# A gated linear attention and a two-layer network on one core: one running sum done by matmuls again, weights loaded in whole quarters, a new order of the work

## The chip, the core and the metric

The kernel runs on one NeuronCore of a Trainium2 chip. The core has five engines that run side by side, each with its own instruction queue: TensorE (PE in the profile, with its weight loads PEld), VectorE (DVE), ScalarE (ACT), GpSimd (POOL) and SyncE (SP), which here only issues DMAs. An instruction waits at the head of its queue until what it needs is there, and holds up whatever is queued behind it. The metric is device time in microseconds, lower is better.

## The reference

For each of 4 batches and 8 heads a state of 48 x 48 is decayed and updated along 768 steps; the result, put together to 3072 rows of 384, goes through two layers.

```python
f = 1 / (1 + exp(-f_logit))                       # q, k, v, f_logit: 4 x 8 x 768 x 48, float32
for t in range(768):
    state = f[:, :, t, :, None] * state + einsum('bhd,bhe->bhde', k[:, :, t], v[:, :, t])
    y[:, :, t] = einsum('bhd,bhde->bhe', q[:, :, t], state)
x = y.transpose(0, 2, 1, 3).reshape(3072, 384)
h = x @ w_in                                      # w_in: 384 x 2048
out = maximum(0.01 * h, h) @ w_out                # w_out: 2048 x 384
```

## The kernel before

The work is cut into twelve units of 256 rows. Units 0 to 3 ("paired") are one batch each, with its first 256 steps, two steps side by side on a partition. Units 4 to 11 are two batches each, with one further chunk of 128 steps. In the names below, a number behind the first one is the half of the unit, or for paired units often the half of the heads.

Attention of a unit: loads `Lf`, `Lk`, `Lq`, `Lv` (SyncE, L164 and L168); `ge` and `gl`, exponential and logarithm on ScalarE (L229, L241), which give the logarithm of the decay; `cs`, its running sum by matmuls with triangles of ones (L250 to L261), followed in a paired unit by four tiny matmuls for the ends; `dec`, exponentials of the running sum with both signs and of its ends (L274 to L280); `k` and `q`, products with these (L286, VectorE or GpSimd as the order's last digit says); then keys and queries are transposed, in units 0 to 2 by TensorE (`tk`, `tq`, L319) and copied out (`ck`, `cq`, L332, L334), in units 3 to 11 by a DMA (`xk`, `xq`, L339). `sc` are the scores (L355, L362), `mk` their mask (L372, L376), `v` the casts of v (L291 to L300), `mx` and `ms` the output with the part that comes from the state (L393), `xt` its copy (L445, L447), `pt` the update of the state (L458, L463), `sf` and `sb` its sums and casts (L473 to L483).

The running sum of a paired unit has two columns of steps. The even one is two matmuls of 192 columns; the odd one is two more, or, for the units in `ADDED`, the even one plus the decay, an addition on VectorE in PSUM (`ca`, L266) ahead of `dec`.

The two layers: `up` (six matmuls of 256 columns for a unit, L510) with `pr` (L516) in units 0 to 3; in units 4 to 11 two units share three matmuls of 512 columns (`uw`, L521, with `pw`, L525). `dn_j_a_n` is a quarter of the second layer for half a unit, four matmuls of 384 columns (L532); `ob` copies the result (L541, L543), `st` stores it. The last unit's second half is done in two halves of columns (`dh`, `oh`, `sh`).

Weights come as quarters of 512 columns (w_in) or rows (w_out) in float32 into four buffers of the raw inputs that units 4 and 5 use later, and are cast to bfloat16. `WI_i` and `WO_i` load quarter i whole, `CI_i_x_e` and `CO_i_x_e` cast a third of it (512 columns of the buffer, on VectorE, ScalarE or GpSimd for e = 0, 1, 2). `We_i_x` loads half a quarter of w_in (256 columns), `Ce_i_x_y_e` casts 128 columns of it. `up_j_g` reads quarter g // 2.

There are eight PSUM banks; the digit behind @ in the order names the bank (or banks) of a TensorE step, and a step waits until the bank's last reader is done. `F_n` are fillers: n matmuls on constants whose result nobody reads.

All of it is issued in one long list of such words, written out from a planner; each engine takes its own words in the order of the list.

Of the kernel before, what the change touches and what calls it, by code (L numbers as in the profile page):

```python
# [15 lines left out]
def kernel(  # L16
# [115 lines left out]
    def fill(n, bank):  # L132
        for _ in range(n):
            nc.tensor.matmul(banks[bank].rearrange("t (a n) -> t a n", a=4), filler,  # L134
                             filler[:, None, :].to_broadcast([128, 4, 128]), start=True, stop=True)
# [452 lines left out]
    sc_0_0@6.2 q_1_1_1 zv_1_1 mk_0_0_0 gl_2_1 F_2@1 cs_2_1@3 q_1_0_0 ca_2_1 F_1@4 tq_1_0@1 dec_2_0 ck_1_0_0 cq_1_0_1
    mk_0_0_1 tq_1_1@4 We_0_0 q_2_0_0 cq_1_1_1 v_1_0 dec_2_1 Lv_2_2 WI_2 F_2@5 sc_1_0@6.7 mx_0_2@5.1 sc_1_1@2.4
    mk_1_0_1 mk_1_0_0 v_1_1 tq_2_0@7 q_2_1_1 mk_1_1_1 mk_1_1_0 xt_0_0_1 ms_0 pt_1_2@3.6 xt_0_1_1 Ce_0_1_0_1  # L590
    Ce_0_1_1_1 F_2@2 mx_1_2@5.4 k_2_0_0 tk_2_0@1 sf_1_0 cq_2_0_0 Ce_0_0_0_1 Ce_0_0_1_1 xt_1_0_1 up_0_1@2 k_2_1_1
    ck_2_0_0 sb_1_0 tq_2_1@3 tk_2_1@7 sf_0_1 v_2_1 v_2_0 We_1_0 up_0_0@1 cq_2_1_1 CI_2_1_2 zs_2_1 ms_1 pr_0_1
# [5 lines left out]
    up_2_7@3 sb_0_1 cs_3_0@0 CO_0_0_2 CO_2_1_2 pr_0_4 CO_2_0_2 gl_3_1 CO_1_2_2 Lf_4_1 CO_1_0_2 pr_2_1 pr_2_2 pr_0_6
    ca_3_0 cs_3_1@7 dec_3_0 pr_2_7 pr_1_6 dn_0_1_0@5 up_2_4@2 up_1_7@6 dn_0_0_0@0 up_2_6@3 Lk_3_2 dn_1_0_0@4 CO_1_1_2
    Lf_5_1 pr_2_4 k_3_0_0 CO_2_2_0 ca_3_1 dec_3_1 Lq_3_2 Lf_5_0 WO_3 dn_0_0_1 q_3_1_1 pr_2_6 CO_3_1_0 k_3_1_1 Lf_4_0  # L600
    dn_1_0_1 dn_1_0_2 dn_0_1_1 dn_1_1_0@2 dn_0_0_2 Lv_3_2 dn_1_1_1 xk_3 sb_1_1 pr_1_7 dn_1_1_2 up_2_5@7 q_3_0_0
    dn_0_1_2 up_0_7@3 CO_3_0_0 v_3_0 sb_2_1 CO_3_2_1 pr_0_7 xq_3 Lq_4_0 v_3_1 Lk_4_0 Lq_5_1 Lk_5_1 Lk_5_0 Lq_5_0
    dn_1_0_3 Lf_6_0 Lf_6_1 Lq_4_1 ob_1_0_0 pr_2_5 ge_4_2 pr_2_0 dn_0_0_3 dn_1_1_3 dn_0_1_3 dn_2_1_0@6 ob_1_1_0
    ob_0_0_0 ge_5_2 gl_5_2 sc_3_1@3.7 sc_3_0@4.1 pt_3_2@2.0 dn_2_1_1 mk_3_0_1 dn_2_1_2 mk_3_0_0 mk_3_1_1 sf_3_0
    mk_3_1_0 cs_5_0@1 dn_2_0_0@4 sb_3_0 cs_5_1@7 dn_2_0_1 dec_5_0 ob_0_1_0 gl_4_2 dec_5_1 mx_3_2@2.1 ms_3 xt_3_1_0
    k_5_2_1 dn_2_0_2 q_5_2_1 Lk_4_1 cs_4_1@3 xk_5 xt_3_0_1 xq_5 up_3_2@5 up_3_5@7 Lv_4_1 pr_3_5 dec_4_1 up_3_6@2
    up_3_1@1 pr_3_1 st_0_0 cs_4_0@7 dec_4_0 ge_6_2 k_4_2_0 sf_3_1 dn_2_0_3 q_4_2_1 Lv_4_0 pr_3_2 up_3_7@3 up_3_0@1
    up_3_4@7 xk_4 pr_3_0 xq_4 up_3_3@0 Lv_5_1 Lv_5_0 sb_3_1 pr_3_6 dn_3_1_0@5 pr_3_3 gl_6_2 Lk_7_1 Lf_7_0 Lq_6_0
    pr_3_4 st_0_1 Lq_6_1 dn_2_1_3 v_4_2 ob_2_0_1 dn_3_1_1 cs_6_0@1 pr_3_7 v_5_2 dec_6_0 Lf_7_1 sc_5_0@2.0 sc_5_1@7.4
    dn_3_1_2 mk_5_0_1 cs_6_1@3 mk_5_0_0 dn_3_0_0@0 dn_3_0_1 st_1_1 mk_5_1_0 sc_4_1@1.2 mk_5_1_1 sc_4_0@7.4 dec_6_1  # L610
    mk_4_1_1 dn_3_0_2 pt_4_0@3 mk_4_1_0 mk_4_0_0 pt_4_1@2 dn_3_1_3 mk_4_0_1 mx_4_1@1 mx_4_0@7 mx_5_1@4 xt_4_1_1
    xt_5_1_1 mx_5_0@1 xt_5_0_1 dn_3_0_3 xt_4_0_0 uw_4_7@7 uw_4_9@4 pt_5_1@1 Lk_6_1 sf_4_1 ob_2_1_1 uw_4_4@2 pw_4_7
    Lf_8_0 Lk_6_0 uw_4_15@6 uw_4_0@7 pw_4_4 sf_4_0 uw_4_10@3 ob_3_1_0 uw_4_3@2 pw_4_9 pw_4_0 q_6_2_1 pw_4_10 ge_7_2
    uw_4_8@4 pt_5_0@7 sf_5_0 uw_4_12@5 uw_4_11@3 pw_4_3 uw_4_1@2 uw_4_2@7 pw_4_15 sb_4_1 gl_7_2 pw_4_8 pw_4_11 xq_6
    Lv_6_1 Lq_7_1 cs_7_1@6 cs_7_0@4 pw_4_1 pw_4_2 dec_7_1 uw_4_6@3 sb_5_0 sb_4_0 Lk_7_0 uw_4_13@2 sf_5_1 Lf_8_1
    Lq_7_0 dec_7_0 pw_4_6 st_1_0 k_6_2_0 pw_4_13 dn_4_1_0@1 uw_4_5@7 xk_6 q_7_2_0 pw_4_5 st_2_1 k_7_2_1 xk_7 Lv_6_0
    xq_7 st_3_1 Lv_7_1 Lv_7_0 ob_3_0_1 Lf_9_0 Lf_9_1 v_6_2 dn_5_0_0@6 dn_4_0_0@4 dn_5_1_0@3 uw_4_14@2 Lq_8_1 ge_8_2
    st_2_0 Lk_9_1 sb_5_1 Lq_8_0 pw_4_12 v_7_2 st_3_0 Lk_8_1 Lq_9_0 Lf_10_0 Lk_8_0 pw_4_14 Lv_9_1 Lq_9_1 gl_8_2
    dn_4_0_1 dn_4_1_1 dn_5_1_1 dn_4_0_2 sc_6_1@7.0 sc_6_0@5.2 Lf_11_1 dn_4_1_2 Lk_9_0 dn_4_1_3 mk_6_1_0 mk_6_1_1
    mk_6_0_1 dn_5_0_1 dn_4_0_3 mk_6_0_0 ob_4_1_0 sc_7_1@7.0 sc_7_0@2.5 cs_8_0@1 dn_5_1_2 dn_5_0_2 Lv_8_1 mk_7_0_1  # L620
    mk_7_0_0 mk_7_1_0 mk_7_1_1 cs_8_1@5 mx_6_1@2 dec_8_1 mx_6_0@7 mx_7_1@0 xt_6_0_0 mx_7_0@5 xt_7_1_0 pt_6_1@7
    xt_6_1_1 xt_7_0_1 sf_6_1 dec_8_0 ge_9_2 sb_6_1 dn_5_0_3 pt_7_0@2 uw_6_14@0 uw_6_0@5 pw_6_0 pw_6_14 gl_9_2
# [58 lines left out]
```

## Time and profile before

| | |
|---|---|
| time, median of 3 runs | 179.84 us (179.12 to 180.2) |
| the profiled execution | 178.5 us, span 176.7 us |
| TensorE busy | 168.0 us, 95% of the span |
| ScalarE, VectorE, GpSimd busy | 107.5, 79.1, 72.7 us |
| HBM read, written | 25.17 MB, 4.72 MB |
| DMA packets | 110,407, of them 102,832 under 512 B |

A row of the page's chain names what the end of the program was waiting for, followed back. A row of groups gives line, engine, operation, tiles, count, busy time and mean nanoseconds of one. A row of the timeline gives start and length in us, and in brackets how long the engine sat idle before it and what ended that. For DMA issues the last number is the time in us from issue to landing.

### The profile page before, as it was taken

How to read it: one execution, taken by the hardware profiler on the slowest of the kernel's cores; microseconds unless marked ns; L12 is line 12 of the kernel's file. 1: busy time of each engine (PE TensorE's matmuls, PEld its weight loads, DVE VectorE, ACT ScalarE, POOL GpSimd, SP SyncE). 2: the span in 40 equal slices, each digit the busy share in tenths (PEclk: the TensorE clock that was granted, in tenths of full speed). 3: DMA queues.
4: the chain of work that ended last, by engine and by line, in shares of the span. 5: the costliest groups of instructions: out<-in, count | busy, mean ns of one | idle time of the engine just before them, and what ended most of it. 6: DMA issues, size and time to landing. Idle time of an engine off the chain costs nothing.

```text
span 176.7 us, 5136 instructions
## 1 busy us (share of the span) xinstructions
PE 168.0 (95%) x2096; PEld 105.6 (60%) x2096; DVE 79.1 (45%) x166; ACT 107.5 (61%) x234; POOL 72.7 (41%) x151
## 2 busy tenths in 40 slices
...
PEclk9999999999999999999999999999999999999999
...
GB/s 148 317 323 342 355 312 353 125 326 209 312 206 210 91 194 177 215 188 200 211 229 233 192 188 216 227 134 212 264 206 225 156 250 0 48 0 137 0 22 156
DMA packets 110407, 34.93 MB, mean 198 GB/s; under 512 B 102832, under 2 KB 109616, under 8 KB 110384
## 3 DMA queue, kind: packets, MB, share of 16 engines
...
HBM read 25.17 MB, written 4.72 MB: 169 GB/s over the span
## 4 chain that ended last, share of the span: by engine, by line
PE 90%; DVE 3%; ACT 2%; DMA 2%; issue 1%; SPq 0%; DVEq 0%
PE ps L532 35%; PE ps L521 22%; PE ps L510 11%; PE ps L393 6%; PE ps L134 3%; PE ps L362 3%; DMA raw_fk<-in_f_logit_dram 2%; PE ps L319 2%; PE ps L548 2%; PE ps L258 1%; DVE wm L372 1%; PE ps L463 1%; PE ps L355 1%; PE ps L458 1%; PE ps L250 1%
## 5 line engine op out<-in xcount | busy, mean ns | idle before, releaser
L532 PE MATMUL ps<-w_out,gT 128*128 128x384 bf16 x368 | 66.1, 326 | 0.9 <-DVE sf L475 0.9
L532 PEld LDWEIGHTS <-gT 128*128 128x128 bf16 x368 | 34.4, 98 | 24.3 <-issue 1.2
L521 PE MATMUL ps<-xT,w_in 128*128 128x512 bf16 x192 | 45.2, 379 | 0.0
L525 ACT ACTIVATE gT<-ps 128x512 bf16<-128x512 f32 x64 | 34.5, 623 | 10.1 <-PE ps L521 9.6
L521 PEld LDWEIGHTS <-w_in 128*128 128x128 bf16 x192 | 18.1, 98 | 18.9
L376 DVE TENSOR_TENSOR wm<-ps,ut 128x512 bf16<-128x512 f32 x32 | 19.9, 684 | 17.0 <-PE ps L362 12.2
L286 POOL TENSOR_TENSOR qh<-raw_qv,at 128x768 bf16<-128x768 f32 (+1 forms) x10 | 14.0, 1404 | 24.3 <-ACT gT L525 9.4
L510 PE MATMUL ps<-xT,w_in 128*128 128x256 bf16 x192 | 22.9, 273 | 0.4 <-ACT xT L445 0.2
L516 ACT ACTIVATE gT<-ps 128x512 bf16<-128x512 f32 x32 | 17.9, 616 | 6.2 <-PE ps L510 6.2
L291 POOL CAST vb<-raw_qv 128x384 bf16<-128x384 f32 (+1 forms) x16 | 11.6, 723 | 23.6 <-DMA raw_qv<-in_v_dram 23.4
L510 PEld LDWEIGHTS <-w_in 128*128 128x128 bf16 x192 | 18.4, 98 | 3.6 <-DVE w_in L189 0.5
L483 POOL CAST sb<-sf 64x192 bf16<-64x192 f32 x40 | 14.9, 374 | 10.8 <-DVE sf L473 8.5
L445 ACT CAST xT<-ps 128x384 bf16<-128x384 f32 x15 | 7.8, 529 | 16.9 <-PE ps L393 13.5
L274 ACT ACTIVATE em<-ps 128x384 bf16<-128x384 f32 x24 | 12.2, 508 | 9.0 <-DVE wm L376 5.5
L229 ACT ACTIVATE e<-raw_fk 128x384 f32<-128x384 f32 (+1 forms) x16 | 11.0, 685 | 8.1 <-DMA raw_fk<-in_f_logit_dram 8.0
L286 DVE TENSOR_TENSOR kh<-raw_fk,em 128x768 bf16<-128x768 f32 (+1 forms) x10 | 9.0, 901 | 14.6 <-ACT em L274 9.7
L475 DVE TENSOR_TENSOR sf<-sf,ps 64x192 f32<-64x192 f32 x32 | 11.2, 351 | 6.4 <-ACT at L275 2.8
L543 DVE COPY osb<-ps 128x384 f32<-128x384 f32 x13 | 7.1, 554 | 13.0 <-PE ps L532 9.0
L275 ACT ACTIVATE at<-ps 128x384 bf16<-128x384 f32 x24 | 12.3, 512 | 0.0
L480 POOL TENSOR_TENSOR sf<-sf,end 128x192 f32<-128x192 f32 x16 | 8.9, 556 | 5.9 <-DVE sf L475 5.6
L372 DVE TENSOR_TENSOR wm<-ps,pair_mask 128x512 bf16<-128x512 f32 x16 | 10.4, 685 | 1.8 <-ACT lf L241 0.9
L134 PE MATMUL ps<-filler 128*128 128x512 bf16 x24 | 9.2, 511 | 2.0 <-DVE filler L93 1.1
(90 smaller groups left out, 180.2 us busy)
## 6 DMA issues: line engine op xcount, KB each, us to landing
...
raw_fk<-in_moe_w_out_dram SPq DMA_DIRECT2D x2, 768.0 KB, 7.2
raw_qv<-in_moe_w_out_dram SPq DMA_DIRECT2D x2, 768.0 KB, 5.0
raw_fk<-in_f_logit_dram SPq DMA_DIRECT2D x3, 384.0 KB, 4.7
```

What stands on the lines that cost most here:

```text
L134: nc.tensor.matmul(banks[bank].rearrange("t (a n) -> t a n", a=4), filler, filler[:, None, :].to_broadcast([128, 4, 128]), start=True, sto ...
L274: nc.scalar.activation(ems[j % 2][:, a], t[:, 0:H * D], AF.Exp, scale=1.0)
L275: nc.scalar.activation(ats[j % 2][:, a], t[:, 0:H * D], AF.Exp, scale=-1.0)
L286: eng.tensor_mul(heads(j, to[j % NR], a)[:, :, :, 0:D], raw_heads(j, x, a), decays(j, by, a))
L372: nc.vector.tensor_mul(w.rearrange("t (s p) n -> t s p n", s=2), src.rearrange("t (s p n) -> t s p n", s=2, p=2), pair_mask[:, :, None, :] ...
L376: nc.vector.tensor_mul(w, src.rearrange("t (p n) -> t p n", p=P2), ut[:, None, :].to_broadcast([128, P2, 128]))
L483: nc.gpsimd.tensor_copy(out=sb[rows, :, y * D:y * D + D], in_=sf[rows])
L510: nc.tensor.matmul(pm[:, i, :], w_in_of(ff, kk), xTs[j // 2 % 2][:, kk, j % 2].rearrange("t a s -> t (a s)"), start=(kk == 0), stop=(kk == ...
L516: nc.scalar.activation(dst, pm, AF.Prelu, alpha=0.01)
L521: nc.tensor.matmul(banks[bank], w_in_of(ff, kk), xTs[j // 2 % 2][:, kk].rearrange("t u a s -> t (u a s)"), start=(kk == 0), stop=(kk == NK ...
L525: nc.scalar.activation(g_blocks(j)[ff], banks[st[j].pop(("pm", ff))], AF.Prelu, alpha=0.01)
L532: nc.tensor.matmul(po, g_of(j, ff, a), w_out_b[quarter][:, ff % 4, :], start=(ff == 0), stop=(ff == NF - 1))
```

## The change

Four things change, and nothing else in the functions:

- `ADDED` loses unit 2: its odd running sums are matmuls again, and the words `ca_2_0` and `ca_2_1` are gone.
- Every quarter of w_in is loaded and cast whole: no `We` and `Ce`, four `WI` and twelve `CI`, in the order 0, 3, 1, 2.
- A filler has 256 columns instead of 512, and there are 35 (16, 8, 4, 5, 2) instead of 24.
- The list is a new one from end to end: other places, other banks, and in part other engines for the copies and products.

```diff
-    ADDED, WIDE = (2, 3), (4, 6, 8, 10)
+    ADDED, WIDE = (3,), (4, 6, 8, 10)
...
-            nc.tensor.matmul(banks[bank].rearrange("t (a n) -> t a n", a=4), filler,
-                             filler[:, None, :].to_broadcast([128, 4, 128]), start=True, stop=True)
+            nc.tensor.matmul(banks[bank][:, 0:256].rearrange("t (a n) -> t a n", a=2), filler,
+                             filler[:, None, :].to_broadcast([128, 2, 128]), start=True, stop=True)
...
-    c0 Lf_0_1 ge_0_1 Lf_1_2 ge_1_1 gl_0_1 ge_1_0 zk_0 zv_0_0 zs_0_0 Lv_0_1 Lf_0_0 F_7@1 cs_0_1@0 ge_0_0 gl_0_0 Lk_0_1
-    Lv_0_0 zk_2 dec_0_1 v_0_1 Lq_0_1 Lk_0_0 Lq_0_0 zk_1 F_3@2 cs_0_0@1 zs_1_0 Lk_1_2 gl_1_0 gl_1_1 k_0_1_0 F_3@3
-    cs_1_0@2 Lf_2_2 dec_0_0 q_0_1_0 k_0_0_0 pm_1 tk_0_1@3 tq_0_1@4 cs_1_1@5 dec_1_0 v_0_0 tk_0_0@6 ck_0_1_0 Lq_1_2
-    Lq_2_2 cq_0_1_0 dec_1_1 Lv_1_2 Lk_2_2 zv_2_0 pt_0_2@7.0 q_0_0_1 sc_0_1@1.3 k_1_0_1 ge_2_0 We_0_1 tq_0_0@2 k_1_1_1
...
-    xt_1_1_1 ut Ce_1_0_0_2 ck_2_1_0 sc_2_0@5.0 sc_2_1@3.7 sf_1_1 pr_0_0 mk_2_1_0 CI_2_0_1 pt_2_2@2.6 CI_2_2_0
-    up_1_1@4 mk_2_0_1 sf_2_0 up_1_0@1 mk_2_1_1 Ce_1_0_1_1 pr_1_1 pr_1_0 mk_2_0_0 up_0_5@3 up_1_5@0 We_1_1 Lf_3_2
-    sb_2_0 WI_3 up_1_4@2 up_0_2@4 mx_2_2@7.1 WO_0 CI_3_1_2 ms_2 xt_2_1_0 Ce_1_1_1_0 xt_2_0_1 up_1_2@5 up_0_4@7
-    Ce_1_1_0_0 pr_1_5 pr_1_2 WO_2 pr_1_4 CI_3_2_2 zs_3_0 ge_3_0 pr_0_2 WO_1 up_0_3@1 ge_3_1 CI_3_0_0 up_2_3@0
...
-    uw_6_6@6 pw_6_6 pw_6_13 dn_6_1_0@7 pw_6_8 uw_6_10@0 dn_6_0_0@2 uw_6_9@6 uw_6_7@4 dec_9_1 pw_6_5 q_9_2_0 q_8_2_1
-    xk_8 xq_8 k_9_2_0 xk_9 pw_6_10 uw_6_11@5 pw_6_11 pw_6_7 pw_6_9 dn_7_1_0@1 dn_7_0_0@3 uw_6_15@0 Lv_9_0 xq_9
...
+    c0 zs_0_1 Lf_0_1 Lf_0_0 zv_0_0 Lf_1_2 Lv_0_0 Lv_0_1 Lk_0_1 ge_0_1 gl_0_1 ge_0_0 zk_1 zk_2 zs_1_1 zk_0 Lq_0_1
+    gl_0_0 pm_1 ge_1_0 ge_1_1 F_16@1 cs_0_1@0 Lq_0_0 dec_0_1 k_0_1_0 cs_0_0@1 dec_0_0 Lk_0_0 gl_1_1 F_8@3 tk_0_1@2
+    gl_1_0 q_0_1_0 v_0_0 v_0_1 F_4@4 cs_1_0@3 tq_0_1@4 cs_1_1@5 k_0_0_1 zv_2_1 Lk_1_2 Lf_2_2 cq_0_1_1 dec_1_0 dec_1_1
+    Lq_1_2 ck_0_1_0 q_0_0_0 zv_1_1 k_1_0_1 tk_0_0@6 ck_0_0_0 k_1_1_1 tq_0_0@7 sc_0_1@0.1 pt_0_2@2.4 cq_0_0_0 mk_0_1_1
+    sc_0_0@6.3 sf_0_0 ge_2_0 ge_2_1 mk_0_1_0 Lv_1_2 q_1_1_0 F_5@7 tk_1_1@7 gl_2_0 tk_1_0@1 gl_2_1 sb_0_0 Lk_2_2
+    ck_1_0_1 cs_2_0@5 v_1_0 v_1_1 q_1_0_0 cs_2_1@2 tq_1_1@0 ck_1_1_1 tq_1_0@1 Lq_2_2 mk_0_0_1 cq_1_1_1 sc_1_1@7.3
+    mk_0_0_0 cq_1_0_1 sc_1_0@0.6 dec_2_1 WI_0 F_2@1 mx_0_2@1.2 mk_1_1_1 mk_1_1_0 dec_2_0 k_2_0_0 xt_0_0_1 k_2_1_1
+    ms_0 tk_2_1@3 q_2_0_1 tk_2_0@7 pt_1_2@5.1 mk_1_0_1 mk_1_0_0 xt_0_1_1 sf_1_0 tq_2_0@2 WI_3 ck_2_0_1 cq_2_0_0
+    mx_1_2@6.7 q_2_1_1 ck_2_1_1 sb_1_0 tq_2_1@0 xt_1_0_1 CI_0_1_1 cq_2_1_0 sc_2_0@3.5 ms_1 sc_2_1@2.6 Lv_2_2 CI_0_0_0
+    CI_0_2_2 mk_2_0_1 mk_2_1_1 mk_2_1_0 CI_3_2_0 WI_1 zs_2_1 v_2_1 v_2_0 xt_1_1_1 sf_1_1 mk_2_0_0 sf_0_1 CI_3_0_1
+    CI_3_1_1 up_0_1@0 up_1_1@7 up_0_0@5 Lf_3_2 pr_0_1 up_1_0@6 pr_1_0 up_1_7@2 up_0_7@0 up_1_6@1 CI_1_0_0 CI_1_2_2
+    pr_1_7 up_0_6@6 WI_2 pr_1_6 Lk_3_2 pr_1_1 pt_2_2@3.2 mx_2_2@4.1 WO_0 CI_1_1_1 ge_3_1 gl_3_1 up_0_2@7 sf_2_0
+    sb_2_0 WO_3 xt_2_0_0 up_1_3@3 ms_2 up_1_2@4 pr_0_0 WO_1 xt_2_1_0 up_0_3@5 up_2_3@1 CO_0_0_2 CO_0_2_2 CO_0_1_2
+    pr_0_7 CI_2_1_0 sf_2_1 up_2_2@0 CI_2_0_1 CI_2_2_0 CO_3_1_2 ge_3_0 pr_0_2 pr_0_6 pr_2_2 pr_1_3 cs_3_1@2 up_1_4@7
...
+    ob_5_1_0 uw_6_4@1 uw_6_0@7 cs_9_1@0 pw_6_4 pw_6_0 pw_6_1 cs_8_1@2 uw_6_13@1 uw_6_5@5 uw_6_11@7 sf_6_1 cs_8_0@3
+    cs_9_0@6 dec_9_1 dec_8_1 uw_6_12@0 uw_6_6@2 dec_8_0 dec_9_0 pw_6_13 Lq_9_1 pw_6_6 pw_6_11 pw_6_5 uw_6_15@3
+    uw_6_2@6 pw_6_2 uw_6_9@1 uw_6_7@2 uw_6_8@7 uw_6_14@5 dn_7_0_0@6 pw_6_10 pw_6_7 dn_7_1_0@4 dn_6_1_0@2 q_8_2_0
+    st_4_1 pw_6_14 dn_7_0_1 sb_6_1 dn_6_1_1 Lv_8_1 xq_8 k_8_2_0 q_9_2_1 Lv_8_0 xk_8 dn_6_0_0@5 k_9_2_0 pw_6_9 pw_6_15
+    pw_6_8 sb_7_0 xq_9 Lf_10_1 Lv_9_1 sc_8_1@1.3 pw_6_12 sc_8_0@7.0 xk_9 mk_8_0_0 mk_8_1_1 mk_8_0_1 dn_7_0_2 dn_6_1_2
+    Lv_9_0 dn_7_0_3 dn_6_0_1 dn_6_1_3 dn_6_0_2 sb_6_0 mk_8_1_0 st_5_1 Lf_11_1 v_8_2 sc_9_1@7.3 sc_9_0@0.1 mk_9_1_0
+    Lq_10_0 Lf_10_0 dn_7_1_1 Lq_11_0 st_4_0 st_5_0 mk_9_1_1 v_9_2 ge_11_2 mk_9_0_1 mk_9_0_0 dn_6_0_3 dn_7_1_2
+    dn_7_1_3 Lk_11_1 mx_8_0@7 mx_8_1@3 Lk_11_0 xt_8_0_0 mx_9_0@1 xt_8_1_0 xt_9_0_0 mx_9_1@0 gl_11_2 ob_6_1_1 pt_8_1@2
+    ob_7_1_1 pt_8_0@4 Lv_11_1 Lk_10_0 sf_8_0 cs_11_1@7 xt_9_1_1 pt_9_0@3 sf_9_0 sf_8_1 uw_8_14@1 cs_11_0@0
```

More of the change, by code (lines that the diff above doesn't have):

```diff
@@ L588 @@
[L588 to L592, printed above, removed]
@@ L598 @@
[L598 to L602, printed above, removed]
@@ L603 @@
[L603 to L622, printed above, removed]
@@ L623 @@
-    uw_6_4@7 dn_5_1_3 uw_6_1@1 ob_5_1_0 pw_6_1 uw_6_8@5 cs_9_0@0 uw_6_3@3 pt_6_0@1 pw_6_4 sf_7_0 uw_6_2@2 ob_4_0_0
-    pt_7_1@7 sf_6_0 uw_6_12@4 pw_6_3 pw_6_12 ob_5_0_1 uw_6_5@3 dec_9_0 cs_9_1@1 pw_6_2 uw_6_13@4 k_8_2_0 sf_7_1
-    uw_6_6@6 pw_6_6 pw_6_13 dn_6_1_0@7 pw_6_8 uw_6_10@0 dn_6_0_0@2 uw_6_9@6 uw_6_7@4 dec_9_1 pw_6_5 q_9_2_0 q_8_2_1
-    xk_8 xq_8 k_9_2_0 xk_9 pw_6_10 uw_6_11@5 pw_6_11 pw_6_7 pw_6_9 dn_7_1_0@1 dn_7_0_0@3 uw_6_15@0 Lv_9_0 xq_9
-    pw_6_15 sb_6_0 sb_7_1 dn_6_0_1 sb_7_0 dn_6_0_2 dn_6_1_1 sc_8_1@5.4 sc_8_0@6.0 dn_7_1_1 mk_8_1_1 Lv_8_0 Lf_10_1
```

60 lines of the change are left out of this document (40 added, 20 removed).

## The prediction

> **What bounds the kernel now.** First the page of the profile: its span, the busy shares and the chain of work that ended last.
>
> ```profile
> span 176.7 us, 5136 instructions
> PE 168.0 (95%) x2096; PEld 105.6 (60%) x2096; DVE 79.1 (45%) x166; ACT 107.5 (61%) x234; POOL 72.7 (41%) x151
> PEclk9999999999999999999999999999999999999999
> PE 90%; DVE 3%; ACT 2%; DMA 2%; issue 1%; SPq 0%; DVEq 0%
> ```
>
> TensorE (PE) is the bound: 90% of the chain. What an order can change is the time in which PE waits, runs fillers, or does work late at the start. So the second view is the list of PE's waits, the third the chain in order of time.
>
> ```profile
> PE ps L250 <- ACT lf L241: 1.6, 1, 1.6
> PE ps L532 <- DVE sf L475: 0.9, 1, 0.9
> PE ps L510 <- DVE w_in L189: 0.2, 1, 0.2
> ```
>
> ```profile
> 4.81 0.52 ACT e L229
> 5.33 0.42 ACT lf L241
> 5.80 0.32 PE ps L250
> 6.12 0.16 PE ps L251
> ...
> 10.08 0.08 PE ps L251
> ...
> 17.68 0.35 PE ps L355 x16
> ...
> 19.11 0.33 PE ps L319 x4
> ...
> 25.94 0.45 PE ps L458 x16
> ...
> 30.42 1.08 PE ps L393 x73
> ...
> 33.05 6.07 PE ps L510 x54
> ...
> 116.86 1.95 PE ps L532 x12
> 118.81 0.55 PE ps L362 x16
> ```
>
> The reader is to see three stages. Until 33.05 us PE works with holes: the first running sum waits for a logarithm until 5.80, and the last hole ends at 33.05, when up_0_3 gets the second half of weight quarter 1 (cast on VectorE, L189). From there PE runs without a gap, except 0.9 us at 110 us, to the end. So a gain can come from the start and from that one wait; a loss from new waits in the long dense part. The median of the runs shown is 179.84 us. The profiled execution took 178.5 us, 1.8 us more than its span; I make the sum against it and carry the difference over to the median. About 0.5% (0.9 us) is what a measurement of this kernel can tell from no change.
>
> **The start.** The new order is worth most if it reaches the dense part with more behind it. I follow the slowest thing that it still needs, the loads.
>
> ```profile
> 1.05 3.17 PE L134 MATMUL ps<-filler 128*128 128x512 bf16 x7 [1.05 <-DVE filler L93]
> 3.43 0.52 ACT L229 ACTIVATE e<-raw_fk 128x384 f32<-128x384 f32 x1 [1.42 <-DMA raw_fk<-in_f_logit_dram]
> 11.68 1.15 SPq L164 DMA_DIRECT2D raw_fk<-in_k_dram  x1
> raw_fk<-in_k_dram SPq DMA_DIRECT2D x1, 384.0 KB, 6.4
> 12.87 1.68 SPq L180 DMA_DIRECT2D raw_fk<-in_moe_w_in_dram  x2
> raw_fk<-in_moe_w_in_dram SPq DMA_DIRECT2D x2, 384.0 KB, 6.3
> 15.13 2.51 SPq L173 DMA_DIRECT2D raw_fk<-in_moe_w_in_dram  x1
> raw_fk<-in_moe_w_in_dram SPq DMA_DIRECT2D x1, 768.0 KB, 8.2
> L286 POOL TENSOR_TENSOR qh<-raw_qv,at 128x384 bf16<-128x384 f32 x4 | 3.7, 918 | 5.3 <-ACT end L277 5.3
> L334 DVE COPY qT<-ps 128x512 bf16<-128x512 bf16 x3 | 1.3, 418 | 0.0
> ```
>
> Opening: ge_0_1 starts at 3.43, but its logarithm gl_0_1 is queued behind ge_1_1 and starts only after 4.81 + 0.42. The new order puts gl_0_1 directly behind: logarithm at 3.9, running sum at about 4.5, where 16 fillers of 256 columns end (7 of 512 take 3.17 us with the last one's latency in it, about 0.43 each, so 16 of half the width take 3.4, from 1.05). That is 1.3 us earlier. The fillers fall from 12,288 columns to 8,960, all in front of operations that wait for other engines anyway: I take nothing for them, and 0.3 us at most if a filler of F_8 or F_4 overruns its wait.
>
> Unit two: its running sums become four full matmuls per half instead of two, 4 x 0.08 = 0.32 us more on PE, standing where PE waits for gl_2_0 and gl_2_1 on ScalarE; without that cover it costs 0.3. The two additions leave VectorE, and dec_2 no longer waits for them. Taken at nothing.
>
> Loads decide what follows. In both orders the 15th load is the last of the attention's ahead of the weights, with the same bytes before it: Lk_2_2 now, issued at 11.68 and landing 6.4 later, at 18.1; Lq_2_2 in the new order. From it: q_2_0 and q_2_1 on GpSimd, 2 x 0.92, to 19.9; tq_2_1 and its copy, 0.3 + 0.42, to 20.7; sc_2_1 0.35. The whole quarter 0 has landed when both halves have now: the second is issued at about 14.0 and lands some 6.3 later, so 20.3; its three casts, each about as long as the copy above, run on three engines until about 21.3. So up_0_1 starts at about 21.4. Quarters 3, 1 and 2 follow in byte order; the whole quarter issued now at 15.13 lands at 23.3, and the same byte count puts 3 at 22.4, 1 at 25.6 and 2 at 28.6, each before the first up that reads it (up_1_7 at 24, up_0_2 at 27.8, up_1_4 at 32). Ups cost 6.07/9 = 0.67 us. To the end of up_2_2: 14 ups 9.4, pt_2 0.45, mx_2 with ms_2 1.08, so 21.4 + 10.9 = 32.3. Before had 10 ups done at 33.05, with the same attention; the lead is 4 x 0.67 + 0.75 = **3.4 us**. [...]
>
> Casts of whole quarters (12 of 512 columns instead of six of those and eight of 384) end up on engines with idle time; nothing. SyncE gets a shorter list (two loads fewer) and doesn't wait for casts of half quarters ahead of the output weights.
>
> [...] A running sum of 192 columns takes 0.16 us at 6.12 and 0.08 at 10.08, though the granted clock of the page reads 9 throughout. By the rows alone the full rate comes at about 10 again. [...]
>
> **The dense part.** Here the rows of the one wait, and of SyncE's queue behind it.
>
> ```profile
> 109.09 0.96 DVE L286 TENSOR_TENSOR kh<-raw_fk,em 128x768 bf16<-128x768 f32 x1 [1.94 <-DMA raw_fk<-in_k_dram]
> 110.08 0.73 DVE L475 TENSOR_TENSOR sf<-sf,ps 64x192 f32<-64x192 f32 x2
> 110.90 1.60 SPq L339 DMA_TRANSPOSE kT<-kh  x1
> 119.55 0.57 SPq L168 DMA_DIRECT2D raw_fk<-in_f_logit_dram  x1
> 123.21 0.84 ACT L229 ACTIVATE e<-raw_fk 128x768 f32<-128x768 f32 x1 [5.71 <-DMA raw_fk<-in_f_logit_dram]
> 124.08 0.84 ACT L241 ACTIVATE lf<-e 128x768 bf16<-128x768 f32 x1
> 124.52 0.87 SPq L567 DMA_DIRECT2D out_dram<-osb  x1
> 129.43 1.71 SPq L168 DMA_DIRECT2D raw_qv<-in_q_dram  x2
> L274 ACT ACTIVATE em<-ps 128x384 bf16<-128x384 f32 x24 | 12.2, 508 | 9.0 <-DVE wm L376 5.5 <-PE ps L261 2.2 <-PE ps L255 0.6
> ```
>
> k_8 waits on VectorE for its load; behind it stands sf_7_1, which frees the bank that dn_6_1_0 needs. In the new order sf_7_1 comes long before, and sf_6_1 stands ahead of q_8. So this 0.9 us goes.
>
> What is late next is the same stretch. The new order puts the exponentials dec_8_0 and dec_9_0 only 12 groups of four or three matmuls (0.65 each, 1.95/3) ahead of sc_8_1; before they lay eleven ups further forward. sc_8_1 comes at 118.81 - 3.4 - 0.9, less one down quarter that the new order has after it, so at 113.9; dec_8_0 then starts at 106, ends about 107.3 behind a relu (two exponentials of 0.51), and q_8 (0.96) ends at about 108.4. Behind q_8, SyncE's queue has xq_8, Lv_8_0, xk_8, xq_9, Lf_10_1, Lv_9_1, xk_9, Lv_9_0, st_5_1 and then Lf_11_1. Now four transposes and two loads take 119.55 - 110.90 = 8.65 us; two more loads (0.86 each) and a store (0.87) make 11.2. Lf_11_1 is issued at 119.6, lands 3.7 later (119.55 to 123.21) and ge_11, gl_11 (0.84 each, behind them on ScalarE are copies of outputs and xt_9_1) end at 125.1. cs_11_1, which now stands directly behind pt_8 in front of nearly all of uw_8, would come at 113.9 + 9.7 = 123.6 (ten down quarters and the first uw_8 and cs between, at these rates). PE then waits in all 1.5 us, part of it already at sc_8 and sc_9 for the transposes; what waits with it is all of uw_8. In general PE waits as long as xq_8's issue is after 106.9. Bounds: 0, and 5.5 (rival two). I take **1.5**.
>
> Sum: -3.4 - 0.9 + 1.5 = -2.8: 175.7 for the profiled execution, 177.0 for the median.
>
> **Rivals.** One: no new wait, because SyncE gets to xq_8 early. 179.84 - 4.3 = 175.5. For it: PE had only one wait after 33.05. Against: the new order's closer transposes.
>
> Two, on the other side: the stream of loads sets the pace at units 8 to 11. Place: xq_8 in SyncE's queue; price: one us per us after 106.9; it decides from 111.2 on, where the wait eats the whole 4.3. If the stream gets there no earlier than to xk_8 now (110.90) and one transpose later (1.60), xq_8 goes at 112.5, PE waits 5.5 and the time is 179.84 - 4.3 + 5.5 = 181.0. For it: SyncE's issues fill the stretch from 110.90 to 119.55, so the stream has no slack there. Against: the stream now has a hole, while SyncE waits for the casts of half quarters:
>
> ```profile
> 31.00:33.00 2.00, 1.86 (x38) 1.27 (x24) 1.41 (x4) 1.80 (x4) 1.28 (x3) 1.00 0.54 200
> 33.00:36.00 3.00, 2.96 (x27) 2.65 (x28) 2.39 (x7) 2.66 (x7) 1.17 (x2) 1.00 0.56 131
> ```
>
> The last two columns are the share of the DMA engines and GB/s: half of five microseconds is unused, and the new order has whole quarters to load there.
>
> Three: the weights are late. Whole quarters come as one landing; if quarter 0 lands at 22.3, the lead is 1.5 and the wait in units 8 and 9 stays, since the loads are then late too, and half a microsecond longer: 179.84 - 1.5 - 0.9 + 2.0 = 179.4, no change that can be told.
>
> [...]
>
> That the change doesn't do what it says I see no room for: the additions of unit two are no longer in the order.
>
> **Chances.** Forecast 0.42, rival one 0.17, two 0.22, three 0.15, four 0.04. Faster by over 0.5%: 0.42 + 0.17 + 0.04 = 0.63; within 0.5%: 0.15; slower: 0.22. The range goes from 174.9 (no new wait, and 0.6 more at the start) to 181.0, the time of rival two; beyond it lie half of that rival and a little below. The cases on the faster side alone span 174.9 to 178.8.
>
> **What would show it.** Right: the first running sum at 4.5; up_0_1 near 21.4; no wait of PE between 21.4 and 40; no wait of a down matmul for sf at 110; a wait at L258, L362 or L521 near 114 to 125 of about 1.5, with ScalarE waiting for the load of f. Wrong: PE waiting at L510 for w_in beyond 22 (rival three), or xq_8 issued after 111 (rival two), or long waits in a place not named here, above all units 4 to 7, whose transposes also stand closer to their scores.

## The result and the profile after: slower by 2.9%

Before 179.48 us (median of 4 runs, 178.87 to 180.2), after 183.43 us (4 runs, 182.53 to 183.65): a ratio of 1.029, 95% interval 1.024 to 1.035. The forecast was 177.0, with a range from 174.9 to 181.0, so both its sign and its range were wrong. A second set of after gave 183.19 beside 179.56, a ratio of 1.016 (1.009 to 1.024). The ratios leave out runs over 1.5% above the fastest of the same kernel; in one set (e9 to e11) a single run of before at 176.73 leaves out nine of thirteen that way, so for it plain medians stand beside the ratio.

The profiled execution took 183.25 us, with a span of 181.5. The page of the kernel after, its span, TensorE's busy line and the clock:

```profile
span 181.5 us, 5159 instructions
PE 168.6 (93%) x2111; PEld 107.6 (59%) x2111; DVE 82.8 (46%) x158; ACT 108.0 (60%) x235; POOL 71.5 (39%) x154
PEclk9999978999999999999999999999999999999999
```

TensorE (PE) is busy for the same time as before (168.0), in a span that is 4.8 us longer, so it waits more. Two slices of the clock read 7 and 8 where before read 9. The list of PE's waits (total, times, longest) says where the time is:

```profile
PE ps L393 <- issue: 3.7, 1, 3.7
PE ps L319 <- DVE kh L286: 1.8, 1, 1.8
...
PE ps L393 <- POOL vb L291: 0.8, 1, 0.8
PE ps L362 <- DMA kT<-kh: 0.8, 1, 0.8
PE ps L258 <- ACT lf L241: 0.5, 1, 0.5
```

The largest wait is one of 3.7 us for nothing that the profile shows ("issue"). The timeline of PE puts it inside the mixing of unit 1, mx_1_2: sixteen matmuls of one kind, four ahead of the stop and twelve behind it. In the same view the first running sum stands at 4.52, as forecast, and the first up at 26.26.

```profile
4.52 0.24 PE L250 MATMUL ps<-lf,bu 128*128 128x192 bf16 x1
...
20.20 0.28 PE L393 MATMUL ps<-wm,v 64*32 64x128 bf16 x4
24.18 0.32 PE L393 MATMUL ps<-wm,v 64*32 64x128 bf16 x12 [3.70 <-issue]
...
26.26 2.57 PE L510 MATMUL ps<-xT,w_in 128*128 128x256 bf16 x13
```

Behind the stop the granted clock is halved for 3.4 us. These rows of the windows give length, then for PE, its weight loads (PEld), VectorE, ScalarE and GpSimd busy time and instructions, and at the end clock, DMA share and GB/s:

```profile
21.50:24.90 3.40, 0.72 (x27) 0.51 (x29) 0.04 (x1) 0.34 (x1) 1.13 (x4) 1.00 1.04 341
24.90:28.30 3.40, 3.40 (x54) 2.30 (x47) 3.31 (x7) 2.85 (x6) 2.24 (x7) 0.50 1.09 361
28.30:31.00 2.70, 2.70 (x27) 2.39 (x26) 2.12 (x6) 0.93 (x3) 0.00 (x0) 1.00 1.08 353
```

In the window with the stop PE is busy for 0.72 of 3.4 us; in the next one it runs at 0.50, which by an estimate from that row (half of 3.4 us, PE busy throughout) costs 1.7 us; then at full rate again (1.00).

To compare kernels with different orders I summed, for every matmul of the work (fillers count nothing), the mean time from its start to the next one's behind 30 us, and read off each trace when as much of that work is left. Eight matmul records that some traces lack were put back by aligning the lists. "Late" below is against before's profiled run: with as much work left as before has at 39 us (some 137 us by these means), and at the last matmul.

| profiled run | late at 39 us | late at the end | lost behind it |
|---|---|---|---|
| after, e5 (after again) | 2.4, 4.1 | 4.8, 5.6 | 2.4, 1.5 |
| e1, e2 (fillers 512, 128) | 2.9, 1.8 | 4.4, 1.8 | 1.5, 0.0 |
| e3, e11 (before's order) | 3.9, 2.3 | 6.05, 2.5 | 2.2, 0.2 |
| e4, e7, e10, e12 (held load) | 1.45, 0.0, -1.3, 1.3 | 3.8, 2.9, 0.1, 3.5 | 2.35, 2.9, 1.4, 2.2 |
| e6, e8, e9 | 3.5, 3.2, 2.1 | 5.0, 6.8, 3.5 | 1.5, 3.6, 1.4 |
| e13, e14, e15 (lighter stream) | 0.75, 3.6, 2.0 | -0.45, 4.0, 1.1 | -1.2, 0.4, -1.0 |

So after, in its first profile, is 2.4 us late where the forecast had it 3.4 early, and loses as much again in the dense part.

### The profile page after: what moved, and what is told of

Same layout as the page of the kernel before. It is cut to its first block, busy times and chain, and to the rows that moved or that the text cites. A ratio compares the mean times of both kernels' runs of the same rounds, so it can differ in the third digit from the quotient of the medians.

```text
span 181.5 us, 5159 instructions
## 1 busy us (share of the span) xinstructions
PE 168.6 (93%) x2111; PEld 107.6 (59%) x2111; DVE 82.8 (46%) x158; ACT 108.0 (60%) x235; POOL 71.5 (39%) x154
## 3 DMA queue, kind: packets, MB, share of 16 engines
HBM read 25.17 MB, written 4.72 MB: 165 GB/s over the span
## 4 chain that ended last, share of the span: by engine, by line
PE 67%; ACT 9%; issue 8%; SPq 5%; DMA 5%; POOL 3%; DVE 0%; POOLq 0%
PE ps L532 25%; PE ps L521 18%; PE ps L510 12%; PE ps L393 5%; SPq L168 3%; DMA out_dram<-osb 3%; ACT gT L525 3%; DMA raw_fk<-in_f_logit_dram 2%; PE ps L362 2%; POOL vb L291 1%; PE ps L258 1%; SPq L339 1%; PE ps L355 1%; ACT em L274 1%; ACT at L275 1%
## 5 line engine op out<-in xcount | busy, mean ns | idle before, releaser
L532 PE MATMUL ps<-w_out,gT 128*128 128x384 bf16 x368 | 64.7, 326 | 0.0
L532 PEld LDWEIGHTS <-gT 128*128 128x128 bf16 x368 | 34.6, 98 | 23.2 <-ACT gT L525 0.2
L525 ACT ACTIVATE gT<-ps 128x512 bf16<-128x512 f32 x64 | 33.9, 639 | 6.9 <-PE ps L521 6.7
L376 DVE TENSOR_TENSOR wm<-ps,ut 128x512 bf16<-128x512 f32 x32 | 19.9, 684 | 19.6 <-PE ps L362 14.7
L510 PE MATMUL ps<-xT,w_in 128*128 128x256 bf16 x192 | 23.1, 280 | 0.0
L516 ACT ACTIVATE gT<-ps 128x512 bf16<-128x512 f32 x32 | 17.6, 619 | 5.2 <-PE ps L510 3.4
L510 PEld LDWEIGHTS <-w_in 128*128 128x128 bf16 x192 | 18.8, 100 | 3.0 <-issue 0.2
L483 POOL CAST sb<-sf 64x192 bf16<-64x192 f32 x40 | 13.8, 346 | 14.0 <-DVE sf L473 11.9
L480 POOL TENSOR_TENSOR sf<-sf,end 128x192 f32<-128x192 f32 x16 | 9.8, 615 | 20.7 <-DVE sf L475 20.3
L543 DVE COPY osb<-ps 128x384 f32<-128x384 f32 x10 | 5.6, 556 | 27.2 <-PE ps L532 24.2
L286 POOL TENSOR_TENSOR kh<-raw_fk,em 128x384 bf16<-128x384 f32 (+1 forms) x10 | 12.0, 1206 | 13.8 <-DMA raw_fk<-in_k_dram 7.8
L286 DVE TENSOR_TENSOR qh<-raw_qv,at 128x384 bf16<-128x384 f32 (+1 forms) x12 | 12.0, 1016 | 10.3 <-ACT at L275 7.2
L445 ACT CAST xT<-ps 128x384 bf16<-128x384 f32 x12 | 6.1, 529 | 15.8 <-PE ps L393 15.7
L541 ACT COPY osb<-ps 128x384 f32<-128x384 f32 x13 | 6.2, 488 | 13.9 <-PE ps L532 12.0
L393 PE MATMUL ps<-wm,v 64*32 64x128 bf16 (+1 forms) x256 | 8.4, 219 | 3.8 <-issue 3.7
```

Of the source, the lines that this page charges most:

```text
L286: eng.tensor_mul(heads(j, to[j % NR], a)[:, :, :, 0:D], raw_heads(j, x, a), decays(j, by, a))
L376: nc.vector.tensor_mul(w, src.rearrange("t (p n) -> t p n", p=P2), ut[:, None, :].to_broadcast([128, P2, 128]))
L393: nc.tensor.matmul(banks[st[j]["py", i]][32 * r:32 * r + 32, 128 * kk:128 * kk + 128], lhsT, rhs, start=(i, r) not in begun, stop=i in las ...
L483: nc.gpsimd.tensor_copy(out=sb[rows, :, y * D:y * D + D], in_=sf[rows])
L510: nc.tensor.matmul(pm[:, i, :], w_in_of(ff, kk), xTs[j // 2 % 2][:, kk, j % 2].rearrange("t a s -> t (a s)"), start=(kk == 0), stop=(kk == ...
L516: nc.scalar.activation(dst, pm, AF.Prelu, alpha=0.01)
```

## The experiments

**Theory 1.** PE's own instructions would come over the DMA engines in pieces, delayed by the load queue, and PE would have to stop at a fixed number of its instructions until the piece lands. **Theory 2.** A wait for an operand is hidden in mx_1_2. **Theory 3.** The loss lies in the dense part.

The windows from 0 to a time inside the stop count what PE issued ahead of it. Before, which stops too, for 0.45 us (first its row of the timeline, then the window):

```profile
23.88 0.33 PE L319 MATMUL ps<-ident,qh 128*128 128x128 bf16 x3 [0.45 <-issue]
...
0.00:23.60 23.60, 19.22 (x351) 12.01 (x352) 15.99 (x45) 17.10 (x41) 16.24 (x52) 1.00 1.02 296
```

After:

```profile
0.00:22.00 22.00, 16.51 (x351) 12.61 (x352) 12.66 (x33) 16.22 (x40) 17.36 (x55) 1.00 0.96 274
```

Both stop behind 351 matmuls and 352 weight loads, 703 instructions, at different work. Packets of 16 KB of a queue of their own (kind "instruction") are in both traces, 16 in all (0.26 MB); PE has 4222 matmuls and weight loads in after. There none comes between 17.3 and 21.7 us; the second starts at 21.76, and PE goes on 2.4 us later. The DMA view of 21.7 to 22.8:

```profile
q1 hardware_dynamic: 661, 0.28, 95.9%
q8 instruction: 1, 0.02, 5.4%
q14 instruction: 1, 0.01, 1.8%
```

The packet of the other instruction queue, q14, isn't what PE waits for: in before it starts at 25.43, behind PE's going on at 23.88.

**e1, e2, e3: other fillers.** Width and count, nothing else:

```diff
-F_16@1 F_8@3 F_4@4 F_5@7 F_2@1     # after: 256 columns
+F_8@1  F_4@3 F_2@4 F_3@7 F_1@1     # e1: 512 columns, 18 fillers
+F_32@1 F_16@3 F_8@4 F_10@7 F_4@1   # e2: 128 columns, 70 fillers
-F_7@1 F_3@2 F_3@3 F_4@5 F_2@1 F_1@4 F_2@5 F_2@2     # before: 512 columns
+F_14@1 F_6@2 F_6@3 F_8@5 F_4@1 F_2@4 F_4@5 F_4@2    # e3: 256 columns, 48 fillers
```

> The kernel after with its fillers 512 columns wide again, at half the count (8, 4, 2, 3, 1 in place of 16, 8, 4, 5, 2): 17 matmuls fewer on TensorE with the same columns, so 34 rows of weight load and matmul fewer. Theory 1 (TensorE's own instructions arrive in pieces over the DMA engines, and the piece behind row 703 lands near 24 us whatever the work is): TensorE stops behind row 703 again, 17 matmuls later in the work, the stop is shorter (about 3.0 us in place of 3.70, perhaps too short for the half clock), time 181 to 182.6. Theory 2 (a wait for an operand hidden in the mixing of unit 1): the stop stays at the same matmul of mx_1_2 with 3.7 us, time as after, 183.4. Theory 3 (the loss lies in the dense part behind 40 us): as after, 183.4.

> The kernel after with fillers of 128 columns, at twice the count (32, 16, 8, 10, 4): 35 matmuls more with the same columns, 70 rows more. Theory 1: TensorE stops behind row 703 again, which now stands 35 matmuls (about 2 to 3 us of work) earlier in the work; the stop is longer, 4.5 us or more, and the time 184.0 to 185.5. Theories 2 and 3: the stop at the same matmul as in after, time 183.4.

> The kernel before with one part of the change alone: fillers of 256 columns at twice the count (48 in place of 24), the order otherwise the one of before; 48 rows more. Theory 1: row 703 is reached 24 matmuls earlier in the work, the stop behind it grows from 0.67 us to about 2, time 180.5 to 181.5. Theories 2 and 3: the same columns, the same time, 179.5.

Windows up to the stop, of e1, e2 and e3 in turn:

```profile
0.00:24.00 24.00, 17.78 (x351) 11.35 (x352) 13.20 (x35) 17.42 (x42) 17.23 (x55) 0.96 0.91 257
```

```profile
0.00:22.00 22.00, 17.04 (x351) 14.51 (x352) 12.60 (x33) 16.47 (x40) 16.27 (x53) 1.00 0.96 271
```

```profile
0.00:22.50 22.50, 17.39 (x351) 13.68 (x352) 15.39 (x42) 16.62 (x40) 14.87 (x47) 1.00 0.98 272
```

All three stop behind 351 and 352. Less the fillers, after has 316 matmuls of the work behind it at the stop, e1 333, e2 281; e1 stands in sc_2_0, e2 in mx_1_2 earlier than after, e3 in mx_1_2, 24 matmuls earlier than before. The count decides, not the work: theory 2 falls. In all four (with before) PE goes on 2.25 to 2.5 us after the start of the instruction packet (packet at 21.63, 22.71, 20.89, 21.18; PE at 23.88, 25.23, 23.34, 23.61).

The times: e1 182.4 (ratio 1.011, 1.003 to 1.019), e2 182.47 (1.011, 1.001 to 1.021), e3 184.28 (1.019, 1.009 to 1.030), before 181.1. e3, above the 180.5 to 181.5 expected, is one part of the change alone, taken at nothing in the prediction; it makes before's order 3.9 us late at 39 us in the profiled run, through a stop of 2.1 us and a clock of 0.84, 0.50 and 0.81 in the three 4 us from 20 to 32. e1's time came as expected (181 to 182.6), though its stop of 1.6 us was shorter than the 3.0 expected and the clock was lower for longer than in after all the same (0.74, 0.50 and 0.90 in the three 4 us from 20 to 32). e2 did not: it should have been slower than after. Its stop did come 35 matmuls earlier in the work, but was shorter (2.2 us), with the packet at 20.89. When the packet starts moves by over a microsecond between these kernels, and by 0.4 us between the two runs of after (21.76, and 22.16 in e5); what moves it isn't shown. In the new order fillers of 512 and of 128 columns took the same time (182.4 and 182.47).

**e4, e7, e10: the first weight quarter held.** A memset of one column of the staging buffer on GpSimd makes the load wait, so that the DMA engines are empty ahead of the next packet of the instruction queue:

```diff
+    def hold(i):
+        nc.gpsimd.memset(staging(i)[:, 0:1], 0.0)
+        "hw": hold,
-... dec_2_1 WI_0 F_2@1 mx_0_2@1.2 ... k_2_1_1
+... dec_2_1 F_2@1 mx_0_2@1.2 ... k_2_1_1 hw_0 WI_0       # e4
# e7: as e4, fillers of 512 columns, 8, 12, 2, 3, 1
# e10: as e7, but v_1_0 v_1_1 hw_0, and WI_0 at its old place
```

> The kernel after with the load of the first weight quarter (WI_0) held back: a memset of one column of its staging buffer on GpSimd behind the key copy k_2_1_1 goes ahead of it, so that the load and the three loads queued behind it start near 18 us in place of 13.5, and the DMA engines run empty before that. The output is the same. Theory 1: the piece of instructions behind row 703 is fetched earlier, near 19 to 20 us in place of 21.8 to 24.2, the stop shrinks from 3.70 us to under 1, the clock isn't halved, and what remains is the later landing of the quarter (25 in place of 20.9 us): time 179 to 182. Theory 2 and 3: the stop stays or grows with the late weights, 183.4 or more.

> The kernel after with the held load of the earlier run (the first weight quarter behind the key copy k_2_1_1) and, against the idle stretch near 7 us, fillers of 512 columns again, in counts 8, 12, 2, 3, 1: 26 in place of 35, 18 rows fewer, TensorE idle under 1 us ahead of the first transposes. Theory 1: the clock isn't halved from 8.8 to 15.6 as it was in the earlier run, the fetch starts near 19 to 20 us, the stop behind row 703 is under 1 us and the clock stays full; what is left is the late weight quarter: 1.5 to 3 us under after, about as before. If a late quarter alone decides: as after.

> The run with the held weight quarter and the long fillers again, but the hold stands on GpSimd behind the value copy v_1_1 (about 17 us) and not behind k_2_1_1 (18.1), so that the load goes out about 1 us earlier, just as TensorE asks for its next piece of instructions. Theory 1 and the stream (behind 40 us the stream of loads sets the pace; in the earlier run it stood 1 to 2.4 us behind the one of before, and the lead of 2.2 us that TensorE had at 30 us was lost by 87): the stop behind row 703 stays under 1 us, the stream comes about 1 us earlier, and the time falls by about 1 us under the earlier run with the hold (183.2 median, 181.4 in its profiled run). If the stream does not matter: the same time as that run.

The DMA view of e10 from 17 to 19.6 us, GB/s in 40 slices: empty engines, then the packet among the first bytes.

```profile
GB/s 41 18 24 18 6 0 0 0 0 0 0 0 0 95 158 63 63 95 95 32 95 32 126 189 126 347 95 95 221 347 378 284 347 378 378 347 378 315 347 315
...
q8 instruction: 1, 0.02, 2.1%
```

It starts at 18.65 (after: 21.76), and PE goes on at 20.90. Its waits in the start:

```profile
PE ps L393 <- issue: 0.7, 1, 0.7
...
PE ps L510 <- DVE w_in L202: 0.6, 1, 0.6
```

The stop shrinks from 3.7 to 0.8 (e4), 0.3 (e7) and 0.7 us (e10), and the clock isn't halved behind it (1.00 from 24 to 28 us in all three). e4 had a lower clock elsewhere (a mean of 0.57 between 8 and 16 us), behind a wait of 2.3 us for kh up to 9.2; the fillers of e7 and e10 bridge that (in e7 the wait is 0.2 us and the clock 1.00 from 8 to 40). So the stop fits theory 1. The hold makes the weights late in turn (the wait at L510 above). The times: e4 182.2 (1.010, 1.005 to 1.016), e7 183.19 (1.017, 1.011 to 1.024), e10 180.53 beside 179.98 by plain medians (ratio 1.010, 1.004 to 1.017). e7 gained nothing over after, against its expectation of 1.5 to 3; its profiled run, 181.41 at a clock of 0.998, was its fastest, and the other three ran at 0.981 to 0.991. e10 is the fastest of the new order's kernels with full loads, and still not faster than before: its profiled run leads by 1.3 us at 39 us, not by 3.4, and ends level. (The leads of 2.2 and 3 us that some expectations name for e7 and e10 were read before the missing records were put back; they are 0 and 1.3.)

**e6 and e9: what the early clock and the halved clock are worth.** e6 drops the first 16 fillers; e9 puts 12 of 512 columns ahead of mx_1_2 and holds no load.

```diff
-... ge_1_1 F_16@1 cs_0_1@0          # after
+... ge_1_1 cs_0_1@0                 # e6
-mx_1_2@6.7
+F_12@6 mx_1_2@6.7                   # e9, other fillers as in e1
```

> The kernel after, unchanged, beside the kernels of this set. All theories: 2 to 3% over before; its stop behind row 703 and a halved clock in the window behind it, as in its first profile.

> The kernel after without its first 16 fillers (those ahead of the first running sum), 32 rows fewer. The clock then opens some us later than at 4.5. Theory 1 (TensorE's instructions set a floor near 24 us): an early clock buys nothing, the floor behind row 703 stays, and 32 rows fewer stand in front of it, so the same work is reached later but the stop is shorter: time 0.5 to 2 us under after. Rival (the recorded one: the early clock is worth 3.4 us and something else ate it): the time is 1 to 3 us above after.

> The kernel after, no load held, with fillers of 512 columns at half the count (36 rows in place of 70) and 12 more of them (24 rows, about 2.6 us at full clock) right ahead of the mixing of unit 1 (mx_1_2), in which TensorE stopped. They use up part of the time in which TensorE would stand still anyway, so no wait of the floor is removed; only the clock should stay full. Theory 1 with the floor: row 703 is still passed near 24 us, the stop behind it is 0.5 to 1.5 us, the clock isn't halved behind it, and the time is 1 to 2 us under after (which stands 1.6 to 2.9% over before), the lost clock of after alone. If the half clock costs nothing (hidden by the weights' landing): as after. If fillers only add work: 2.6 us over after.

e5, the same kernel again, stopped in its profiled run for 3.3 us in mx_1_2, at a mean clock of 0.979 over the run (after: 0.991). e6: 183.08 (1.018, 1.011 to 1.024) beside after's 183.19 in the same set. Without the first fillers the running sums reached their full rate later: in e6 they still start 0.16 us apart at 11.51 to 11.98, and 0.08 apart only at 15.41. But neither the gain that theory 1 gave nor the loss that the recorded lead would bring came; as 32 instructions went with the early full rate, the run doesn't part the two. e9: 181.61 beside 179.98 (plain medians 0.9% apart, ratio 1.013, 1.009 to 1.017). Its window behind the stop:

```profile
24.00:28.00 4.00, 3.14 (x98) 2.14 (x87) 2.13 (x5) 2.50 (x6) 2.26 (x7) 1.00 1.02 309
```

PE goes on at 25.17, no earlier than in after, but at full clock (in after 0.61 in these 4 us). The time is 1.6 to 1.8 us under after's, as expected, but that isn't shown to be the bridge: e1, with the same wide fillers and no bridge, stood no further from its own before (0.7% by plain medians, ratio 1.011), and the two ran in different sets. What e9 shows is work that nobody reads, put into a wait that came anyway, with a full clock behind it (1.00 from 24 to 28 us; e1, with the same wide fillers and no bridge, had 0.50), at no cost that these times tell. (Its own halved window came between 8 and 12, mean clock 0.59, behind the wait for kh.)

**e11: a late PE in before's order.**

```diff
-mx_1_2@5.4 k_2_0_0 tk_2_0@1
+mx_1_2@5.4 k_2_0_0 F_12@1 tk_2_0@1
```

> The kernel before with 12 fillers of 512 columns (24 rows, about 2.6 us at full clock) put on TensorE behind the mixing of unit 1, near 24 us, and nothing else changed: TensorE's work is late by about 2.6 us from there, the loads already in the queue are not. If the stream of loads alone paces the dense part: much of the delay is caught up, time 0 to 1.5 us above before. If TensorE and the stream go in lockstep (its results free the buffers and copies that the next loads wait for): 2 to 3.5 us above before; the dense part then gives back nothing of a late start and may add to it, as in the kernel before with narrow fillers (late by 3.6 us at 30, by 6.0 at the end).

The run shows the cleanest stop of all, in PE's timeline:

```profile
21.75 2.11 PE L134 MATMUL ps<-filler 128*128 128x512 bf16 x9
24.67 0.38 PE L134 MATMUL ps<-filler 128*128 128x512 bf16 x1 [0.82 <-issue]
```

PE stops between fillers, which read constants and write a bank that nothing reads between them, again behind 351 matmuls. In the profiled run 2.3 us late at 39 us became 2.5 at the end, but that isn't lockstep: before's wait of 0.9 us for sf is gone from its list, so that much was caught up, and a new stop of the same kind took most of it away, in the mixing of units 4 and 5. e1 has one there too (e11's row first):

```profile
78.22 0.23 PE L393 MATMUL ps<-wm,vb 128*32 128x128 bf16 x3 [0.64 <-issue]
...
79.56 0.23 PE L393 MATMUL ps<-wm,v 128*32 128x128 bf16 x2 [1.07 <-issue]
```

They stand in the middle of like matmuls, behind 2238 and 2236 instructions. So PE stops for "issue" in the dense part as well, in some runs. The plain medians, 181.54 and 179.98, are 1.6 us apart, between the two expectations.

**e8 and e12: waits of the dense part, one at a time.** e8 moves the value loads of units 4 and 5 ahead of three transposed loads; e12 is e10 with a log ahead of an output copy on ScalarE.

```diff
-xq_5 xq_4 up_3_6@6 ... xk_4 up_3_7@5 dn_3_1_0@2 Lv_4_1 Lv_4_0 Lv_5_1 Lv_5_0
+Lv_4_1 Lv_4_0 Lv_5_1 Lv_5_0 xq_5 xq_4 up_3_6@6 ... xk_4 up_3_7@5 dn_3_1_0@2    # e8
-sf_7_0 ob_4_0_1 gl_8_2
+sf_7_0 gl_8_2 ob_4_0_1                                                         # e12
```

> The kernel after with one thing moved in the dense part: the four value loads of units 4 and 5 stand ahead of the three transposed loads xq_5, xq_4 and xk_4 in SyncE's queue, in place of behind them. The stop at 20 us is left as it is. If the wait of 0.8 us for unit 4's values at 77 us is a cost of its own: 0.8 to 1.2 us under after. If later waits swallow it: as after. Theory 1 alone says nothing of it.

> The last kernel with the held quarter (its time 180.5, median, beside 180.0 of before) with two words of ScalarE's queue exchanged: the log of unit 8 (gl_8_2) ahead of the copy ob_4_0_1, which waits 2.05 us there for a store to leave its buffer while TensorE waits 0.79 us for the log at 105 us. If TensorE and the stream go in lockstep, a wait of TensorE in the dense part is paid for in full: 0.7 to 1 us less, 179.5 to 179.9, about 0.3% under before. If the stream paces it alone: the next load is waited for instead, the same 180.5.

e8 is the slowest kernel of all, 186.7 (1.037, 1.031 to 1.044). The wait for the values is gone from its list; one for a transposed load took its place, more than twice as long, with a clock of 0.70 behind it (73 to 76 us):

```profile
PE ps L362 <- DMA qT<-qh: 1.9, 1, 1.9
PE ps L362 <- DMA kT<-kh: 0.7, 1, 0.7
```

In e12 the wait for the log at 105 us is gone, and no other came at that place. Its time, 181.07 (1.016, 1.011 to 1.020), doesn't show it: the start of its profiled run was 2.6 us later than that of e10, and that is more than the wait. This one stays undecided.

**e13, e14, e15: a lighter stream of loads.** Half of the heads in the query and value loads, 3.1 of 34.6 MB less, for before, after and e10. (The expectations say units 3 to 11; unit 3's loads have the paired form and stay whole, so it is 4 to 11.)

```diff
+                n = H // 2 if x in "qv" else H
-                queue.dma_start(out=raw(j, x)[:, a],
-                                  in_=srcs[x][2 * h + a, :, c * C:(c + 1) * C, :].rearrange("h t d -> t h d"))
+                queue.dma_start(out=raw(j, x)[:, a, 0:n],
+                                  in_=srcs[x][2 * h + a, 0:n, c * C:(c + 1) * C, :].rearrange("h t d -> t h d"))
```

> The kernel before with a lighter stream: the query and value loads of units 3 to 11 bring the first four of eight heads only (half of 192 or 384 KB; the copies read older data for the rest, so the output isn't the reference's), some 3 MB of 34.6 less. Everything else, TensorE's work above all, is as in before. If the stream of loads paces the dense part: 0.5 to 1.5 us under before, for TensorE has few waits for loads there. If the engines pace themselves: as before, within 0.5.

> The kernel after with the same lighter stream (half of the heads in the query and value loads of the units behind the first three). The start, its stop and its half clock are as in after. If the stream paces the dense part: the 2.2 us that after lost behind 30 us go, 181 to 181.5, and the distance to the lighter kernel before is the one at 30 us, 2 to 2.5 us. If waits among the engines do it: as after, 183.3.

> The kernel with the quarter held behind v_1_1 and the long fillers (180.5, level with before; TensorE leads by 3 us at 30 us) with the same lighter stream. If the stream paces the dense part: the lead now lasts to the end, 177 to 178, 2 to 3 us under the lighter kernel before. If waits among the engines take the lead away: 180 to 180.5, level with the lighter before.

The times: 178.44 (0.995, 0.990 to 1.000), 182.6 (1.022, 1.015 to 1.030) and 179.89 (1.006, 1.001 to 1.012), beside 179.1. The waits of PE between 40 and 170 us go: in e13 and e15 that list is empty; before had 0.9 (for sf), e10 had these:

```profile
PE ps L258 <- ACT lf L241: 0.8, 1, 0.8
PE ps L393 <- POOL vb L291: 0.7, 1, 0.7
```

e14 keeps of after's 2.1 us these:

```profile
PE ps L363 <- DMA kT<-kh: 0.8, 1, 0.8
PE ps L259 <- ACT lf L242: 0.2, 1, 0.2
```

In the table the dense part is 1.1 to 2.4 us shorter with the lighter stream. But the starts of e14 and e15 came out 1.2 and 3.3 us later than in the profiled runs of after and e10 (for e15 with a stop of 1.3 us, and a mean clock of 0.99 over the run), and so the times of those two fell by no more than before's own. The loads do end waits in the dense part; that they set its pace as a whole isn't shown, and e14 and e15 stayed 1.1 and 1.9 us above the slowest time expected for that.

## Why the prediction was wrong, step by step

**The start, -3.4 us: the step that failed.** Up to 20 us it went as written: the first running sum at 4.52 (forecast 4.5), and mx_1_2 began earlier than before. The running sums were fast from the first on: 0.08 us each from 4.52, where before's took 0.16 at 6.12. (Before's clock records begin only at 9.86 us, after's at 4.41; the 9s of PEclk ahead of them are no measurement.) Then the step counted "the slowest thing that it still needs, the loads", and had nothing for the stop behind instruction 703, which by theory 1 is a wait for one load more, PE's instructions. The loads that it did count came near their times: the first cast of quarter 0 starts at 21.07, where the forecast had the quarter landed at 20.3, and rival three's sign, a wait for w_in, isn't in after's list. But PE passes instruction 703 only at 24.18, in before at 23.88, whatever was gained ahead of it (23.3 to 25.4 us in all kernels without a hold); up_0_1 came at 26.26 instead of 21.4. What turned no gain into 2.4 us of loss is the halved clock behind the longer stop (1.7 us), and that after has more work left at instruction 703 (316 matmuls behind it against before's 327, an estimate of 0.7 us by the means of the table). With the 0.3 us by which it goes on later that makes 2.7, less 0.2 for before's own wait for w_in near 33 us. One of the chances, 0.04, is for 0.4 us less from an early full rate, and the range's lower end has 0.6 us more at the start; no run shows either: after, at full rate from its first running sum, came to up_0_1 later, not earlier, and e6, without its first fillers, took 183.08 beside 183.19.

**"The fillers ...: I take nothing for them": also failed.** Narrow fillers are instructions, each a weight load and a matmul: the 11 more of them and the 4 matmuls more of unit 2's running sums are 30 of the 703. e3 shows the price in before's order, at equal columns; in the new order the widest and the narrowest, e1 and e2, took the same time, so how much of after's loss is theirs stays open.

**Unit two and the casts, taken at nothing.** Not run alone. No wait in the profile belongs to them, except that unit 2's matmuls are among those 703.

**The wait for sf, -0.9: right.** It isn't in after's list.

**The new waits, +1.5: near in size by luck, wrong in place.** PE waits 2.1 us in all. None is at sc_8, sc_9 or cs_11, and none is in the list behind 111 us; sc_8_1 runs at 122.33 without a wait. They are at units 5, 6 and 8: for values whose loads stand behind four transposes (78.10), for xk_6 (98.01), and for the log gl_8_2, behind an output copy that waits for a store (110.20). The prediction's last lines named "long waits in a place not named here, above all units 4 to 7" as a sign of error. Against before the dense part lost 2.4 us in the first profile and 1.5 in the second, where the terms made 0.6 (the waits on the lists make 1.2 of the 2.4). xq_8 was issued at 115.10, past the 111 that stood for rival two, but it cost nothing: PE came to sc_8_1 8.4 us later than the 113.9 of the sum.

**A lead passes to the end: not shown.** It was assumed, not worked out. e10 leads by 1.3 us at 39 us and ends level, after waits for a log and for values; e11 is 2.3 us late there and 2.5 at the end, with one wait less and one stop more. One profiled run of each isn't enough to say how much of a lead or of a delay the dense part takes.

**What stays open:** how much of the dense part's loss is the new order's own. e3, in before's order, loses 2.2 us there too, and e11 only 0.2.

No version with full loads beat before. Nearest is e10, level by plain medians and 1.0% over by the ratio.
